# Sliding-window attention and a two-layer block on one core: the fourth tile of keys and queries transposed by DMA, and the loads of tiles 4 and 5 issued after two GpSimd copies

## The chip, the core and the metric

The kernel runs on one core of a Trainium2 chip. The metric is the device time of one execution in microseconds; the kernel before has been run eight times, and the median of those runs is what a change is compared with. One further view, the profile, is taken of one of these executions.

## The reference, cut to what matters

```
q, k, v: (8, 8, 576, 64) float32           # batch, heads, sequence, head dimension
scores = q @ k^T / 8, only where |i - j| <= 32, then softmax, then @ v
x = attention output as 4608 tokens x 512
h = x @ w_in                                # 512 -> 2048
g = h * sigmoid(1.702 h)
out = g @ w_out                             # 2048 -> 512
```

## The kernel before, in words

**Units and windows.** The 4608 tokens are one long row, cut into 36 units of 128 tokens. A window w handles two units of attention (2w and 2w+1), the first layer for the units of the window before it (`layer1(w-1, ...)`), and the second layer for the units of two windows before. The order of instructions on every engine is the order in which the program writes them[...]. `head()` is a hand-written start for units 0 to 6, `window(4)` is a written-out transition, and from window 5 on `window(w)` repeats, one window after the other, until `close`. In the steady part the second layer is a Strassen-like set of seven products (`product`, line 394) whose sums are made by VectorE (`g_sums`).

**Keys and queries.** Attention needs keys and queries transposed, head dimension on the partitions: `kT` (a ring of 1536 keys, with 64 wrapped columns behind it, from `RING` on) and `qT` (the same for queries, 384 columns for each of four interleaved positions, with wrapped columns from `RP` on). They come in tiles of 512 tokens: tile 3 is tokens 1536 to 2047, and it lands at the start of the ring again. Its first 64 keys are the last ones that unit 11 needs, and unit 11 reads them from the wrapped columns. There are two ways from DRAM to `kT`:

- By TensorE: `load_heads` (line 138) brings rows of 256 values, `pair_heads` (a `cast`, line 106) puts two heads side by side, `heads_T` (line 176) transposes on TensorE into PSUM, and `keys_T` and `queries_T` copy out of PSUM (line 106 again). Tiles A, B, 1, 2 and 3 go this way.
- By DMA: `load_keys` (line 146) brings rows of 64 values, and `keys_X` (line 151) is a DMA transpose of 128 tokens at a time, from the SyncE queue. For queries `load_heads` and `pair_heads` stay, and `queries_X` (line 221) is one DMA transpose of the whole tile. Tiles 4 to 8 go this way.

**Queues.** All loads with a cast from float32 are issued by GpSimd, in program order: `load_v` (line 157), `load_keys`, `load_heads`. SyncE issues all DMA transposes, the stores of the output (lines 349 and 423), and `x_T` (line 315), the transpose of the attention output that layer 1 multiplies. An instruction that waits on either of these two engines holds all that stand behind it. Staging tiles `ks` and `qs` have three buffers each, `p` five, `xT` four.

**Order around the change.** At the end of `head`, GpSimd copies tile 2 side by side, then loads values 8 to 10, tile 3, values 11 to 13, and tile 4. In window 4 TensorE computes scores 7, 8 and 9, the second layer of units 4 and 5, values 7 to 9, and layer 1 of window 3 (eight pieces), between which stand the transposes of tile 3. `loads()` near the middle brings values 14 and 15 and tile 5. At the end of window 4 and 5 `feed` issues `keys_X(4, ...)`, makes the shifted copies of values (`odd_v`) and, in window 5, the side-by-side queries of tile 4 and `queries_X(4)`. Window 6 starts with `loads()` for tile 6.

Of the kernel before, what the change touches and what calls it, by code (L numbers as in the profile page):

```python
# [22 lines left out]
JT = 4  # L23
NV = 8
RING = 1536
RP = RING // JT


class _Kernel:
# [410 lines left out]
    def head(self):  # L440

        nc, dve, act, pool = self.nc, self.nc.vector, self.nc.scalar, self.nc.gpsimd
# [125 lines left out]
        self.load_v(8)  # L568
        self.load_v(9)
        self.load_v(10)  # L570
        for c in "kq":
            self.load_heads(3, c)
        self.layer1(2, 0)
        self.values(6)
        self.norm(6)
# [13 lines left out]
            self.odd_v(m, dve)  # L589
        for m in (11, 12, 13):  # L590
            self.load_v(m)
        self.load_keys(4)
        self.load_heads(4, "q")

    def window(self, w):
        nc, dve, sp = self.nc, self.nc.vector, self.nc.sync
        a, b = 2 * w, 2 * w + 1
        att = w < self.NW
        t, act = w - 2, nc.scalar
        l1 = [(lambda d=d: self.layer1(w - 1, d)) for d in range(8)] if w <= self.NW else []  # L600

        def run(lst, n=1):
            for _ in range(min(n, len(lst))):
                lst.pop(0)()

        def loads():
            for m in (2 * w + 6, 2 * w + 7):
                if m < self.NU:
                    self.load_v(m)
            if w % 2 == 0 and 512 * (w // 2 + 3) < self.N:  # L610
                self.load_keys(w // 2 + 3)
                self.load_heads(w // 2 + 3, "q")

        if w == 4:
            l2 = [(lambda u=u, i=i: self.layer2(u, i, "oh"[u % 2], (dve, act)[u % 2])) for u in (4, 5) for i in range(4)]
            self.scores(7)
            self.scores(a)
            run(l2, 3)
            self.band(7)
            self.scores(b)  # L620
            run(l2)
            self.band(a)
            self.values(7, "th")
            self.gelu_table()
            for m in (10, 11):
                self.odd_v(m, act)
            self.band(b)
            self.norm(7)
            run(l2, 2)
            self.values(a)  # L630
            self.values(b)
            run(l2)
            self.x_T(7, "t", nc.scalar)
            self.norm(a)
            self.x_T(a)
            self.norm(b)
            self.x_T(b)
            run(l2)
            loads()
            run(l1, 2)  # L640
            for c in "qk":
                for hp in range(4):
                    self.pair_heads(c, 3, hp, dve)
            run(l1, 2)
            for hp in range(4):
                self.keys_T(3, hp)
                self.queries_T(3, hp, "a", nc.scalar)
                run(l1)
            self.g_sums(w - 1, 0)
            self.feed(w)  # L650
            return
        loads()
        if not att:
            self.close(w, l1)
            return
        self.scores(a)
        if w > 5:
            self.scores(b)
        self.g_sums(t, 1, (0, 1))
        self.product(t, 1, "o")  # L660
        self.keep(t, 1, dve)
        self.product(t, 2, "h")
        if w == 5:
            self.scores(b)
        self.g_sums(t, 1, (2, 3))
        self.result(t, 11)
        self.gelu_table()
        self.product(t, 5, "t")
        self.band(a)
        self.product(t, 6)  # L670
        self.band(b, 0)
        self.keep(t, 6, dve)
        self.band(b, 1)
        run(l1)
        self.values(a)
        self.values(b)
        self.norm(a)
        self.x_T(a)
        self.product(t, 7)
        self.keep(t, 7, dve)  # L680
        self.result(t, 22)
        run(l1, 1)
        self.product(t, 4)
        self.result(t, 21, act)
        self.norm(b)
        self.x_T(b)
        self.product(t, 3)
        self.result(t, 12)
        run(l1, len(l1) - 4)
        self.g_sums(w - 1, 0)  # L690
        self.feed(w)
        run(l1, 4)
# [36 lines left out]
    def feed(self, w):  # L729

        dve = self.nc.vector
        if w % 2 == 0:
            self.queries_wrap((w + 2) // 2)
        for m in (2 * w + 2, 2 * w + 3):
            if 11 < m < self.NU:
                self.odd_v(m, dve)
        i = (w + 4) // 2
        if 512 * i < self.N:
            if w % 2:
                if 512 * i % RING == 0:  # L740
                    dve.tensor_copy(self.kT[:, :, RING:], self.kT[:, :, 0:64])
                for hp in range(4):
                    self.pair_heads("q", i, hp, dve)
                self.queries_X(i)
            for c in ((2, 3) if w % 2 else (0, 1)):
                self.keys_X(i, c)
        if w == 16:
            dve.tensor_copy(self.kT[:, :, RING:], self.k_first)
            dve.tensor_copy(self.qT[:, :, RP:RP + 8], self.q_first)

    def run(self):
        self.head()
        for w in range(4, self.NW + 2):
            self.window(w)
# [47 lines left out]
```

## Time and profile before

| | |
|---|---|
| median of 8 runs | 297.7 us (295.8 to 300.29) |
| the execution that was profiled | 300.29 us, span 298.4 us |
| TensorE matmul busy | 288.4 us, 97% of the span |
| VectorE, ScalarE, GpSimd busy | 195.3, 189.6 and 86.8 us |
| DMA, all queues | 37.78 MB, 118,650 packets |
| time of one steady window | 14.61 us (from the scores at 129.08 to those at 143.69) |

The profiled execution is the slowest of the eight, so what it shows of stalls need not be in every run. Busy time of an engine is the time in which an instruction of it ran; a transfer's landing time is counted from its issue to the last byte's arrival. "SPq" is SyncE as the issuer of transfers, and a line such as `L106` is shared by every copy of the kernel, so it is told apart by the tiles that it writes and reads.

### The profile page before, as it was taken

The numbers are of one execution on the slowest core, as the hardware profiler recorded it, in microseconds if no ns is written. First come the engines' busy times: TensorE is split into PE (matmuls) and PEld (weight loads), VectorE is DVE, ScalarE is ACT, GpSimd is POOL, SyncE is SP. The second block draws the span as 40 slices with busy tenths as digits, with TensorE's granted clock in tenths as the row PEclk, the third lists the DMA queues.
The fourth block names the chain that finished last, engine by engine and source line by source line (L and its number), as shares of the span: only waits on it lengthen the run. The fifth ranks groups of instructions, "written<-read, shape, count | busy, mean of one in ns | idle before, by whom it ended". The sixth has DMA issues, their size and how long they took to land.

```text
span 298.4 us, 9587 instructions
## 1 busy us (share of the span) xinstructions
PE 288.4 (97%) x4050; PEld 236.9 (79%) x4052; DVE 195.3 (65%) x584; ACT 189.6 (64%) x314; POOL 86.8 (29%) x127
## 2 busy tenths in 40 slices
PE   7999999999999987999999999999999999999995
PEld 2578665866888875888888888888888888888884
DVE  3662468678786754595759686867686758683352
ACT  4676467698866665384849494848585757575330
POOL 8884525967365200902080202011100000000000
PEclk9999999999999998999999999999999999999999
DMA  9999999999999999999499959691953030303012
GB/s 145 156 207 205 200 184 167 159 165 191 124 166 142 166 121 162 119 182 147 124 114 189 161 107 143 90 164 34 141 110 105 2 109 3 108 2 105 2 70 73
DMA packets 118650, 37.78 MB, mean 127 GB/s; under 512 B 96080, under 2 KB 114256, under 8 KB 118608
## 3 DMA queue, kind: packets, MB, share of 16 engines
q0 software_dynamic: 75888, 18.16, 74.5%
q1 hardware_dynamic: 42272, 18.62, 32.8%
q8 instruction: 32, 0.52, 0.8%
q10 hardware_dynamic: 448, 0.39, 0.5%
q14 instruction: 10, 0.08, 0.1%
HBM read 36.96 MB, written 9.44 MB: 155 GB/s over the span
## 4 chain that ended last, share of the span: by engine, by line
PE 90%; DMA 5%; POOL 2%; DVE 1%; issue 1%; ACT 0%; POOLq 0%; DVEq 0%
PE h_ps L332 43%; PE o_ps L394 30%; PE o_ps L344 7%; PE pv L292 4%; PE sc L263 4%; DMA xT<-x 2%; DMA qs<-in_q_dram 2%; PE tp L176 2%; POOL ve L157 1%; PE tp L319 0%; POOL ks L138 0%; DVE o_sb L412 0%; POOL neg L237 0%; DVE kT L106 0%; ACT qT L106 0%
## 5 line engine op out<-in xcount | busy, mean ns | idle before, releaser
L332 PE MATMUL h_ps<-xT,w_in_sb 128*128 128x256 bf16 x1152 | 136.4, 273 | 2.1 <-DMA xT<-x 2.0
L334 ACT ACTIVATE g<-h_ps 128x512 f16<-128x512 f32 x144 | 85.5, 596 | 78.1 <-PE h_ps L332 76.8
L332 PEld LDWEIGHTS <-w_in_sb 128*128 128x128 bf16 x1152 | 112.2, 98 | 16.0 <-issue 2.6
L157 POOL DMA_DIRECT2D ve<-in_v_dram x40 | 33.9, 859 | 100.0 <-PE pv L292 83.9
L394 PEld LDWEIGHTS <-gs 128*128 128x128 f16 x480 | 46.1, 98 | 6.0
L394 PE MATMUL o_ps<-w_sum,gs 128*128 128x256 f16 x360 | 44.8, 275 | 0.0
L269 ACT ACTIVATE p<-sc 128x512 bf16<-128x512 f32 x72 | 37.2, 604 | 2.7 <-PE sc L263 2.5
L394 PEld LDWEIGHTS <-g 128*128 128x128 f16 x360 | 34.2, 98 | 4.5 <-ACT g L334 0.2
L371 DVE TENSOR_TENSOR gs<-g 128x512 f16<-128x512 f16 x30 | 12.7, 422 | 31.6 <-ACT g L334 30.9
L304 DVE TENSOR_TENSOR x<-pv,rec 128x256 bf16<-128x256 f32 x72 | 30.6, 424 | 2.7 <-DVE rec L303 0.2
L394 PE MATMUL o_ps<-w_out_sb,g 128*128 128x256 f16 x240 | 29.1, 273 | 0.0
L106 DVE COPY part<-o_ps 128x256 f32<-128x256 f32 x45 | 19.1, 424 | 13.5 <-PE o_ps L394 12.3
L412 DVE TENSOR_TENSOR o_sb<-o_ps,part 128x256 f32<-128x256 f32 x45 | 19.0, 422 | 12.1 <-PE o_ps L394 11.4
L281 DVE TENSOR_TENSOR p<-p,mask 128x512 bf16<-128x512 bf16 x64 | 24.3, 422 | 0.6 <-ACT p L269 0.6
L344 PE MATMUL o_ps<-w_out_sb,g 128*128 128x512 f16 x96 | 23.2, 380 | 0.0
L106 DVE COPY vo<-ve 64x528 bf16<-64x528 bf16 x61 | 19.0, 312 | 3.1 <-DMA ve<-in_v_dram 1.7
L303 DVE RECIPROCAL rec<-pv 128x4 f32<-128x4 f32 x72 | 12.6, 175 | 12.7 <-PE pv L292 12.5
L146 POOL DMA_DIRECT2D ks<-in_k_dram x22 | 18.8, 874 | 2.4 <-DMA qs<-in_q_dram 1.0
L431 ACT ACT_TABLE_LOAD x15 | 19.2, 1283 | 0.3
L269 ACT ACT_TABLE_LOAD x15 | 19.2, 1283 | 0.3
L292 PEld LDWEIGHTS <-p 128*64 128x64 bf16 x576 | 11.5, 113 | 6.2 <-DVE p L281 3.4
L263 PEld LDWEIGHTS <-kT 64*64 64x64 bf16 x1152 | 11.8, 107 | 5.7 <-issue 5.3
(69 smaller groups left out, 263.6 us busy)
## 6 DMA issues: line engine op xcount, KB each, us to landing
out_dram<-o_sb SPq DMA_DIRECT2D x34, 256.0 KB, 2.8
ve<-in_v_dram POOLq DMA_DIRECT2D x32, 128.0 KB, 6.2
ks<-in_k_dram POOLq DMA_DIRECT2D x19, 128.0 KB, 8.4
w_in_sb<-in_moe_w_in_dram POOLq DMA_DIRECT2D x4, 512.0 KB, 11.1
w_out_sb<-in_moe_w_out_dram POOLq DMA_DIRECT2D x4, 512.0 KB, 12.6
qs<-in_q_dram POOLq DMA_DIRECT2D x2, 448.0 KB, 11.8
qs<-in_q_dram POOLq DMA_DIRECT2D x3, 256.0 KB, 7.3
qs<-in_q_dram POOLq DMA_DIRECT2D x2, 384.0 KB, 13.0
```

The source lines that it names most:

```text
L106: (eng.copy if eng is self.nc.scalar else eng.tensor_copy)(out, in_)
L157: self.nc.gpsimd.dma_start(self.ve[m % NV][off:off + n, :, :self.D], self.v[b, :, s:s + n, :].rearrange("h s d -> s h d"))
L263: nc.tensor.matmul(sc[eo][lo:lo + 64, 2 * hp + blk, :], self.kT[r, hp, at:at + 64], self.qT[r, JT * hp:JT * hp + JT, q0:q0 + 16], start=(s ...
L269: nc.scalar.activation(p[:, eo].rearrange("k h (s j) -> k h s j", j=JT), sc[eo].rearrange("k h (j s) -> k h s j", j=JT), AF.Exp, scale=sel ...
L281: self.nc.vector.tensor_mul(pv, pv, msk.to_broadcast([128, 4, 2, SQ]))
L292: nc.tensor.matmul(acc[half][blk * 64:blk * 64 + 64, hh, :], p[:, h % 2, h // 2 * 2 + blk, :], vt[:, h, :D + 1], start=(hh == 0), stop=(hh ...
L304: nc.vector.tensor_mul(x[:, hs, :], acc[half][:, :, :D], rec[:, hs, :].to_broadcast([128, 4, D]))
L332: nc.tensor.matmul(hps[:, i, :], self.w_in_sb[:, kr, ff * 128:(ff + 1) * 128], self.xT[t][:, kr, :], start=(i == 0 and kr == 0), stop=(i = ...
L334: nc.scalar.activation(self.g[t][:, ffs[0]:ffs[1] + 1:ffs[1] - ffs[0], :], hps, AF.Gelu_apprx_sigmoid)
L344: nc.tensor.matmul(o_ps, self.g[t][:, ff, s * 128:(s + 1) * 128], self.w_out_sb[:, ff, :], start=(ff == 0), stop=(ff == self.NFF - 1))
L394: nc.tensor.matmul(self.part[t, key], x, y, start=(first and k == 0), stop=(k == 7), skip_group_check=True)
L431: self.nc.scalar.activation(self.spark, self.spark, AF.Gelu_apprx_sigmoid)
```

## The change

Tile 3 goes the second way. In `head`, `load_keys(3)` takes the place of `load_heads(3, "k")`, and the four `keys_X(3, c)` stand at the end. The loads of tile 4 leave `head`. In window 4, ScalarE makes the side-by-side queries of tile 3 where it made the shifted values 10 and 11 (VectorE makes those later, where it made the side-by-side keys and queries). SyncE then issues `queries_X(3)`. GpSimd makes the two wrapped copies, of 64 columns of `kT` and 8 of each row of `qT`, and only after them come the loads: values 14 and 15, tile 4, tile 5. The transposes on TensorE of tile 3 and the copies out of PSUM are gone, and `feed(4)` no longer makes the wrapped copy of queries on VectorE.

```diff
@@ head
-        for c in "kq":
-            self.load_heads(3, c)
+        self.load_keys(3)
+        self.load_heads(3, "q")
...
         for m in (11, 12, 13):
             self.load_v(m)
-        self.load_keys(4)
-        self.load_heads(4, "q")
+        for c in range(JT):
+            self.keys_X(3, c)
@@ window: loads()
-            if w % 2 == 0 and 512 * (w // 2 + 3) < self.N:
-                self.load_keys(w // 2 + 3)
-                self.load_heads(w // 2 + 3, "q")
+            for i in ((4, 5) if w == 4 else (w // 2 + 3,) if w % 2 == 0 else ()):
+                if 512 * i < self.N:
+                    self.load_keys(i)
+                    self.load_heads(i, "q")
@@ window 4
             self.gelu_table()
-            for m in (10, 11):
-                self.odd_v(m, act)
+            for hp in range(4):
+                self.pair_heads("q", 3, hp, act)
+            self.queries_X(3)
+            self.nc.gpsimd.tensor_copy(self.kT[:, :, RING:], self.kT[:, :, 0:64])
+            self.nc.gpsimd.tensor_copy(self.qT[:, :, RP:RP + 8], self.qT[:, :, 0:8])
+            loads()
             self.band(b)
...
             run(l2)
-            loads()
-            run(l1, 2)
-            for c in "qk":
-                for hp in range(4):
-                    self.pair_heads(c, 3, hp, dve)
-            run(l1, 2)
-            for hp in range(4):
-                self.keys_T(3, hp)
-                self.queries_T(3, hp, "a", nc.scalar)
-                run(l1)
+            for m in (10, 11):
+                self.odd_v(m, dve)
+            run(l1, 8)
             self.g_sums(w - 1, 0)
             self.feed(w)
@@ feed
-        if w % 2 == 0:
+        if w % 2 == 0 and w > 4:
             self.queries_wrap((w + 2) // 2)
```

## The prediction

> **What bounds the kernel now.** I read the page first, then the chain of waits around the one place where TensorE stops, then the SyncE queue and the DMA shares there.
>
> ```profile
> span 298.4 us, 9587 instructions
> PE 288.4 (97%) x4050; PEld 236.9 (79%) x4052; DVE 195.3 (65%) x584; ACT 189.6 (64%) x314; POOL 86.8 (29%) x127
> ...
> PE   7999999999999987999999999999999999999995
> ...
> PEclk9999999999999998999999999999999999999999
> DMA  9999999999999999999499959691953030303012
> ```
>
> TensorE is full in all slices but the first, the last and two at 112 to 127 us, where its clock dips too. DMA is full until about 149 us. So the kernel is bound by TensorE, and the DMA engines are the threat in the first half. The critical chain from 105 us shows the dip:
>
> ```profile
> 104.92 4.58 PE h_ps L332 x42
> 109.51 7.43 DMA xT<-x
> 116.93 0.14 issue
> 117.07 1.71 PE h_ps L332 x8
> ```
>
> The busy times by stretch, there (TensorE's matmuls, weight loads, VectorE, ScalarE, GpSimd, then granted clock, DMA share, GB/s):
>
> ```profile
> 115.00:117.00 2.00, 0.04 (x1) 0.00 (x0) 0.76 (x2) 0.14 (x1) 0.00 (x0) 1.00 0.93 163
> 117.00:119.00 2.00, 1.93 (x20) 1.26 (x22) 0.00 (x0) 0.19 (x1) 0.00 (x0) 0.57 0.55 122
> 119.00:121.00 2.00, 2.00 (x38) 1.64 (x33) 1.12 (x4) 0.41 (x1) 1.35 (x2) 0.58 0.03 8
> ```
>
> TensorE waits from 115.04 to 117.07 for the transposed x of unit 13, issued at 109.51, and then runs at 0.57 of its clock for some 3.4 us. Window 7 takes 129.08 - 109.55 = 19.53 us instead of 14.61: 4.9 us lost, which includes 1.0 us of waiting for `qT` at 110 us. Why is that transpose late? The SyncE queue:
>
> ```profile
> 70.65 2.70 SPq L315 DMA_TRANSPOSE xT<-x  x2
> ...
> 74.08 5.59 SPq L151 DMA_TRANSPOSE kT<-ks  x2
> 87.04 1.19 SPq L315 DMA_TRANSPOSE xT<-x  x1
> ...
> 89.75 1.28 SPq L315 DMA_TRANSPOSE xT<-x  x1
> ...
> 95.90 6.41 SPq L221 DMA_TRANSPOSE qT<-qc  x1
> 102.40 4.55 SPq L151 DMA_TRANSPOSE kT<-ks  x2
> 107.04 1.74 SPq L315 DMA_TRANSPOSE xT<-x  x1
> ...
> 109.51 1.87 SPq L315 DMA_TRANSPOSE xT<-x  x1
> ```
>
> The queries of tile 4 landed 15.1 us after their issue, and everything behind them slid: the whole string from 95.90 to the last landing took 21.0 us. The DMA counts say what it shared with: from 101 to 112 us GpSimd's queue moved 3024 packets and SyncE's 2762; from 112 to 118 GpSimd's moved 206 and SyncE's 2868. The string caught up only when the loads ran dry.
>
> **What the Trainium skill says.** "DMA: Bandwidth & Descriptors", section "Queues, rings and completion order", says that each DMA engine takes turns between the queues that have work, packet by packet. The trace agrees that the two share: two key transposes beside a full load queue landed after 10.7 us, against 2.5 us for the quickest. The same page, "Anatomy of one DMA", says that a transfer's semaphore wait is held by the issuing sequencer; so a wait of GpSimd or SyncE holds all behind it, as the in-order rows above show. "TensorE: Matmul & The Clock Gate", part 1, gives an idle window of about 3.4 us as what halves the clock; here 2.03 us of idling sufficed and 1.0 us (at 110 us) did not, so the measurement decides, and I price a second long stop at 1.7 us (half of 3.4).
>
> **The change part by part.**
>
> *Removed from TensorE:* the 32 transposes of tile 3, in the chain four pieces "0.45 PE tp L176 x8" between layer-1 pieces: 4 x 0.45 = 1.8 us, all on the path, since TensorE is full there. Certain gain: 1.8 us. Off the path: on VectorE eight side-by-side copies (2.5 us) and eight copies of keys out of PSUM (3.3 us); on ScalarE four of queries (2.3 us). In their place VectorE gets four shifted copies of values (1.3 us) and ScalarE four side-by-side copies for 2.59 us of value copies, nearly equal. VectorE and ScalarE have room in window 4; nothing.
>
> *Added load:* `load_keys(3)` has 512 x 8 = 4096 pieces of 128 bytes where `load_heads` had 1024. Loads of such pieces ran at 2677 packets in 3 us (55 to 58), so 4.6 us against about 3.0 (0.52 MB at the 175 GB/s of 85 to 90 us). GpSimd issues five transfers of 0.88 for two of 0.69 us: 3.0 us more ahead of queries 3 and values 11 to 13. Tile 4's load no longer follows, so these still land by about 68 us, when ScalarE wants the queries (its value copies started at 68.14). Nothing; up to 1 us if they slip.
>
> *Added transposes:* four `keys_X(3)` and `queries_X(3)`, together 4096 packets of 256 bytes. At 2868 packets in 6 us, alone on the engines, 8.6 us of transfer. The keys fall at 60 to 70 us; queries are issued when ScalarE is done, 68.14 + 2.4 = 70.5, with GpSimd's queue dry, and land after 4.3 (best) to 7.3 us (median of `qT`): I take 5, 75.6 us. The x transposes of units 8 and 9 slide from 70.65 to about 73 and are wanted at 84.49 - 1.8. Nothing.
>
> *The new wait:* GpSimd's two copies stand behind these. GpSimd's 128x512 copies took 0.6 us; these have 256 and 128 elements, so an estimated 0.8 for both: done at about 76.5. Scores 11 want them at 82.36 - 1.8 = 80.6: 4 us to spare. Nothing on the path, but queued behind the copies are all loads from value 14 on. At 76.75 GpSimd before had issued everything through keys 5 (72.55 + 4.20). After, it begins there: values 14 and 15 (2.3 us at the 892 per us above), keys 4 (4.6), queries 4 (3.0), keys 5 (4.6), 14.5 us of transfer, of which before still had some 5 to move. So the load queue lags by 9 us from there. The engines idled little before 118 us, so the lag isn't made up by then.
>
> *Where it is paid, first:* `keys_X(4, 0)` and `(4, 1)` wait for keys 4, issued at 78.3 to 80 us and landing near 82 to 84 (2.6 to 5 us for small loads on a fresh queue); before they had been issued at 74.08. Their 1024 packets now stand right ahead of the x of units 10 and 11. From 77 to 85 us SyncE's queue got 1765 packets in 8 us, 221 per us: 4.6 us, until about 87, with x of unit 10 due out at 85.2. So that string is 1.9 us later. Unit 11's x landed at 89.75 + 8.8 = 98.55 against 99.11 when layer 1 wanted it: 0.6 to spare, so 1.3 us of stop. Bounds: 0 (no delay) and 4.0.
>
> *Second:* the string from `queries_X(4)` to unit 13's x. It starts 1.8 earlier with TensorE and 1.9 later by the above. In its last 5 us (112 to 117) it no longer drains alone: some 1850 packets that are left (2868 without the 1024 of the next keys) go at 2762/11 = 251 per us, 7.4 us instead of 5: +2.4. Bounds: 0 and the whole lag, 9. So TensorE resumes at 117.07 - 1.8 + 1.9 + 2.4 = 119.6, 2.5 us later than before, with the first stop contained in that. A second halving of the clock after the first stop, 1.3 us being between the 1.0 that did not and the 2.0 that did: half of 1.7, 0.9. Window 8 has 5 us to spare for its x (issued 123.83, landing 4.2 later, wanted at 133.34): nothing, up to 2.
>
> *Sum:* +2.5 + 0.9 = +3.4 us; 300.29 + 3.4 = 303.7 for the profiled execution. That one lies 2.6 above the median and has the whole 4.9 of window 7, about the width of all eight runs, so other runs lose less there. I carry the difference over: 297.7 + 3.4 = 301.1, say 301.0. A measurement of this kernel can tell about 1% from no change, 294.7 to 300.7.
>
> **The rivals.**
>
> *First, not slower: the transposes keep their turn.* If SyncE's queue gets its share whatever waits in the other, the lag of the loads costs nothing, since they are prefetches, and both stops stay as they were: 297.7 - 1.8 = 295.9. If the gap in the loads at 67 to 76 us lets the strings run freely and window 7's stop goes too, 300.29 - 1.8 - 4.9 = 293.6. For it: x of units 10 and 11 landed in time beside full loads. Against it: queries 4 took 15.1 us, and from 98 to 101 us SyncE's queue got 100 packets of 2975. It decides from the point where unit 13's x lands less than 2 us after TensorE's new want, 113.2.
>
> *Second, slower still: scores 11 wait for the wrapped copies.* If queries 3 land as late as queries 4 did, 70.5 + 15.1 + 0.8 = 86.4 against 80.6: 5.8 us stop, the loads slipping with it, 301.1 + 5.8 = 306.9. For it: a full chain of load, ScalarE, transpose, GpSimd. Against: GpSimd's queue is dry just then.
>
> **How the numbers follow.** Main case 0.50 (of which 0.08 end within 1%), first rival 0.40 (0.13 of it faster by over 1%, 0.27 within), second 0.10. So faster 0.13, same 0.35, slower 0.52. Range: down to 294.0 (the stop gone), up to 306.0 (first stop at its bound, 2.7 more, and 2 of window 8). The main case alone spans 299 to 305.
>
> **What would show it.** Right: no `tp<-ident,kc` after 71 us; window 5's scores begin near 78.4; loads silent between about 67 and 76 us; a wait for xT near 97 us and a longer one near 114. Wrong: unit 13's x landing by 115 with full loads beside it (the share argument fails), a wait of `sc` at 80 us (second rival), or stops in window 4.

## The result, and the profile after

The changed kernel has a median of 306.78 us over 11 runs (301.24 to 310.25), the kernel before 297.4 us over 32. The ratio is 1.0215, with a 95% interval of 1.0154 to 1.0276. It leaves out each kernel's runs that lie more than 1.5% above its fastest, eight of the changed kernel's and the profiled execution of each kernel among them; the two medians take in all runs and lie further apart (1.032). The forecast was 301.0 us, in a range of 294.0 to 306.0. The ratio alone would put the changed kernel at 304.1 us (1.0215 times 297.7), inside the range; the median of all its runs lies above it. The profiled execution took 308.21 us; its page and slices:

```profile
span 306.5 us, 9523 instructions
PE 290.4 (95%) x4018; PEld 237.2 (77%) x4020; DVE 190.5 (62%) x571; ACT 187.6 (61%) x310; POOL 89.6 (29%) x132
...
PE   7989999999999399999599999999999999999995
...
PEclk9979999999999799999969999999999999999999
DMA  9999996999999999999999996793845030303012
```

Where one dip stood in the slices of 104 to 119 us (the prediction read them as 112 to 127), there are now two, near 100 and near 150 us, each with a dip of the clock at it. A third dip of the clock, at 15 to 23 us, is new too. TensorE's rows at the ends of the two, with the idle time before them and its releaser in brackets:

```profile
104.49 1.87 PE L332 MATMUL h_ps<-xT,w_in_sb 128*128 128x256 bf16 x8 [5.54 <-DMA xT<-x]
...
153.49 1.89 PE L332 MATMUL h_ps<-xT,w_in_sb 128*128 128x256 bf16 x8 [3.70 <-DMA xT<-x]
```

Both wait for an x transpose. The first is that of unit 11, which layer 1 wants in window 6, the second that of unit 17, wanted in window 9. Eight matmuls took 1.87 us where such a row takes 1.04 (before, at 75.20): the granted clock is 0.50 from 104.40 to 106.40 us, and again from 153.40 to 155.40.

A table of windows, each from the start of its first scores on TensorE's timeline to that of the next, says where the 8.1 us between the two spans lie:

| | before | after | difference |
|---|---|---|---|
| start to scores 7 | 61.55 | 63.22 | +1.67 |
| window 4 | 18.58 | 16.60 | -1.98 |
| window 5 | 14.80 | 14.80 | 0 |
| window 6 | 14.62 | 21.61 | +6.99 |
| window 7 | 19.46 | 14.62 | -4.84 |
| window 8 | 14.61 | 14.61 | 0 |
| window 9 | 14.61 | 20.86 | +6.25 |

They sum to 8.09 us. (The prediction's 19.53 for window 7 took its end from another view.) Windows 6 and 9 lost more than their stops of 5.54 and 3.70 us, and the clock is the rest: behind the two stops it stayed at half until 107.5 and 158.7 us, 3.0 and 5.2 us of TensorE's work, of which half, 1.5 and 2.6 us, is lost.

The start isn't the change's. The clock was at half there from 18.8 to 22.2 us, and 3.4 us at half the clock are 1.7 us. In the fourteen traces of this case, the seven with such a halving near 20 us reach scores 7 at 63.22 to 64.35 us, and the seven without it at 61.55 to 62.38. Three of those without it carry the change (61.69, 61.91 and 62.38), and one of those with it is a kernel whose start and window 4 are those of the kernel before (63.34, the run with the key transposes of every tile later). Its slices of the clock show the dip:

```profile
PEclk9979999999999999999999999999999999999998
```

Why the clock halves there in some executions was not looked into.

The chain in GpSimd's and SyncE's timelines shows how window 6 comes to stop. First GpSimd, with its two copies at lines 629 and 630:

```profile
71.54 0.40 POOL L629 COPY kT<-kT 128x256 bf16<-128x256 bf16 x1 [6.60 <-DMA kT<-ks]
79.93 0.29 POOL L630 COPY qT<-qT 128x128 bf16<-128x128 bf16 x1 [7.98 <-DMA qT<-qc]
80.44 1.76 POOL L157 DMA_DIRECT2D ve<-in_v_dram  x2 [0.22 <-issue]
82.19 3.53 POOL L146 DMA_DIRECT2D ks<-in_k_dram  x4
```

and SyncE:

```profile
71.89 4.52 SPq L221 DMA_TRANSPOSE qT<-qc  x1
76.50 3.56 SPq L315 DMA_TRANSPOSE xT<-x  x2
...
87.48 3.36 SPq L151 DMA_TRANSPOSE kT<-ks  x2
90.94 1.35 SPq L315 DMA_TRANSPOSE xT<-x  x1
...
93.05 1.28 SPq L315 DMA_TRANSPOSE xT<-x  x1
...
95.81 9.27 SPq L221 DMA_TRANSPOSE qT<-qc  x1
```

The queries of tile 3 land 8.0 us after their issue; the engines are not free for them, since values 11 to 13 land from 73.1 to 75.8 us and tile 3's own key transposes from 71.5 to 75.1. The copies end at 80.2, the keys of tile 4 are issued at 82.19 and land 5.2 us later, and so SyncE can't go past `keys_X(4, 0)` before 87.48. The x of units 10 and 11 stand behind it, 3.9 and 3.3 us later than before (87.04 and 89.75), although TensorE was 0.3 us ahead of before there (scores 12 at 94.62 against 94.93). And the x of unit 11 then takes 11.3 us to land instead of 8.8.

### The profile page after: what moved, and what is told of

The parts are those of the page before. It is cut to its first block, busy times and chain, and to the rows that moved or that the text cites. A ratio compares the mean times of both kernels' runs of the same rounds, so it can differ in the third digit from the quotient of the medians.

```text
span 306.5 us, 9523 instructions
## 1 busy us (share of the span) xinstructions
PE 290.4 (95%) x4018; PEld 237.2 (77%) x4020; DVE 190.5 (62%) x571; ACT 187.6 (61%) x310; POOL 89.6 (29%) x132
## 4 chain that ended last, share of the span: by engine, by line
PE 86%; DMA 9%; DVE 2%; ACT 1%; issue 0%; SPq 0%; DVEq 0%
PE h_ps L332 40%; PE o_ps L394 28%; DMA xT<-x 7%; PE o_ps L344 7%; PE pv L292 4%; PE sc L263 4%; PE tp L176 2%; DMA k_raw<-in_k_dram 1%; PE tp L319 1%; DVE x L304 1%; ACT qT L106 0%; PE sc L245 0%; ACT g L334 0%; PE junk L437 0%; DVE kc L106 0%
## 5 line engine op out<-in xcount | busy, mean ns | idle before, releaser
L332 PE MATMUL h_ps<-xT,w_in_sb 128*128 128x256 bf16 x1152 | 138.5, 277 | 9.3 <-DMA xT<-x 9.2
L332 PEld LDWEIGHTS <-w_in_sb 128*128 128x128 bf16 x1152 | 113.5, 99 | 24.6 <-issue 5.8
L371 DVE TENSOR_TENSOR gs<-g 128x512 f16<-128x512 f16 x30 | 12.7, 422 | 35.4 <-ACT g L334 35.4
L146 POOL DMA_DIRECT2D ks<-in_k_dram x27 | 22.8, 874 | 9.2 <-DMA qs<-in_q_dram 4.3
L394 PE MATMUL o_ps<-w_sum,g 128*128 128x256 f16 x120 | 15.6, 272 | 0.0
```

The costliest lines, as they stand in the source:

```text
L146: self.nc.gpsimd.dma_start(kn[off:off + n, c], self.k[b, :, s:s + n, :].rearrange("h s d -> s h d"))
L332: nc.tensor.matmul(hps[:, i, :], self.w_in_sb[:, kr, ff * 128:(ff + 1) * 128], self.xT[t][:, kr, :], start=(i == 0 and kr == 0), stop=(i = ...
L394: nc.tensor.matmul(self.part[t, key], x, y, start=(first and k == 0), stop=(k == 7), skip_group_check=True)
```

## The experiments

Each ran beside the kernel before on the same chip. Ratios have their 95% intervals beside them; "loses" is a window's length less 14.61 us.

### Tile 4 ahead of the copies

```diff
+            for m in (14, 15):
+                self.load_v(m)
+            self.load_keys(4)
+            self.load_heads(4, "q")
             self.nc.gpsimd.tensor_copy(self.kT[:, :, RING:], self.kT[:, :, 0:64])
             self.nc.gpsimd.tensor_copy(self.qT[:, :, RP:RP + 8], self.qT[:, :, 0:8])
-            loads()
+            self.load_keys(5)
+            self.load_heads(5, "q")
```

> The changed kernel, with the loads of values 14 and 15 and of tile 4 ahead of GpSimd's two copies; only tile 5 stays behind them. Theory A (tile 4 comes late, its key transposes hold SyncE's queue, and the x of units 10 and 11 stand behind them): keys 4 land before 80 us, SyncE issues the x of unit 10 near 87 again, and the 5.5 us stop of window 6 falls under 1.5 us; time about 1.00 to 1.01 of before. Theory B (the added transposes and their traffic slow every x transpose, whenever tile 4 is loaded): the stop of window 6 stays at 4 us or more and the time at about 1.02. A price either way: the queries of tile 3 are transposed beside loads and land later than the 8.0 us of the changed kernel, so scores 11 may wait up to 4 us.

Measured: 307.14 us, 1.0369 (1.0296 to 1.0443). SyncE had finished with the keys of tile 4 before it came to the x of unit 10, and window 6 lost 0.35 us: that part of theory A holds. Its time was wrong all the same. The queries of tile 3 landed after 13.6 us, and scores 11 waited for GpSimd's copy:

```profile
86.13 0.41 PE L263 MATMUL sc<-qT,kT 64*64 64x64 bf16 x28 [3.60 <-POOL qT L634]
```

Window 5 lost 5.9 and window 7 8.8 us. With tile 4's loads not held, the loss moves to other windows; it doesn't go.

### Holding alone

```diff
         for m in (11, 12, 13):
             self.load_v(m)
-        self.load_keys(4)
-        self.load_heads(4, "q")
...
                 self.queries_T(3, hp, "a", nc.scalar)
                 run(l1)
+            self.nc.gpsimd.tensor_copy(self.qT[:, :, RP:RP + 8], self.qT[:, :, 0:8])
+            loads()          # tiles 4 and 5, as in the changed kernel
```

The `loads()` further up in window 4 and the wrapped copy on VectorE go.

> The kernel before, tile 3 transposed on TensorE as it was, but tiles 4 and 5 are loaded in window 4 behind one GpSimd copy (the wrapped queries) that waits for ScalarE's last queries of tile 3, near 80 us. Theory A (holding the loads is the cost): windows 6 and 9 stop as in the changed kernel, 5 to 6 us each, and the time is that of the changed kernel plus the 1.8 us of transposes that TensorE keeps: 1.02 to 1.035 of before. Theory B (the added transposes are the cost): no such stop, 0.99 to 1.01.

Measured: 311.41 us, 1.0479 (1.0409 to 1.0549), the slowest of all and above what was expected. The GpSimd copy ran at 82.55, SyncE came to the keys of tile 4 at 90.05, and TensorE stopped in the same two windows:

```profile
106.78 1.89 PE L332 MATMUL h_ps<-xT,w_in_sb 128*128 128x256 bf16 x8 [5.01 <-DMA xT<-x]
...
157.07 1.86 PE L332 MATMUL h_ps<-xT,w_in_sb 128*128 128x256 bf16 x8 [3.94 <-DMA xT<-x]
```

Window 6 lost 7.2 and window 9 6.5 us, against 7.0 and 6.25 in the changed kernel, with no added transpose anywhere. Held loads suffice for both stops. The spans of the two traces are 3.6 us apart (310.1 and 306.5 us), 2.0 of it in window 4, where the transposes stay on TensorE.

### Keys of tile 4 behind the x

```diff
         self.x_T(b)
+        if w == 5:
+            for c in (0, 1):
+                self.keys_X(4, c)
...
-            for c in ((2, 3) if w % 2 else (0, 1)):
+            for c in ((2, 3) if w % 2 else (0, 1) if w > 4 else ()):
```

> The changed kernel, with the first two key transposes of tile 4 issued behind the x of unit 11 instead of ahead of the x of unit 10. Theory A: SyncE issues the x of unit 10 near 87 and of unit 11 near 89.5 instead of 90.94 and 93.05; the stop of window 6 falls from 5.5 to 2 us or less, the stop of window 9 stays; time 1.00 to 1.015 of before. Theory B (shared engines, not the order): x of unit 11 still lands after 102 us, and the time stays at 1.02.

Measured: 303.08 us, 1.0209 (1.0131 to 1.0288). SyncE's timeline has the x at 87.12 and 89.80, as theory A said, and window 6 lost 0.05 us. But window 7 now lost 8.5 us:

```profile
112.03 0.41 PE L263 MATMUL sc<-qT,kT 64*64 64x64 bf16 x28 [1.91 <-DMA qT<-qc]
...
120.09 1.86 PE L332 MATMUL h_ps<-xT,w_in_sb 128*128 128x256 bf16 x8 [4.05 <-DMA xT<-x]
```

and the stop of window 9, which I had expected to stay, was gone. SyncE's order says which window pays. That an amount of transfer is late as a whole behind it is a reading, which this run alone doesn't show. The ratio is that of the changed kernel (1.0215): nothing was gained that the runs can tell.

### Tile 5 at the start of window 5

The loads of tile 5 move from behind tile 4 to the start of window 5.

> The changed kernel, with tile 5 loaded at the start of window 5, behind values 16 and 17, instead of right behind tile 4. Theory A (SyncE's wait for keys 4): x of unit 10 is still issued near 91, and the stop of window 6 shrinks by less than 1.5 us. Theory C (the x of unit 11 lands in 11.3 us because tile 5's keys run beside it): values 16 and 17 are in place of them, nearly the same traffic at that time; if it shrinks by more than 2.5 us, the amount loaded back to back is what counts. Time 1.01 to 1.025.

Measured: 307.62 us, 1.0358 (1.0296 to 1.0421). The x of unit 10 was issued at 91.32, the stop of window 6 was 3.46 us instead of 5.54, between what the two theories said, and window 9 lost 6.8 us. The time is above the expected range: moving tile 5 alone by so little gains nothing.

### The added transposes alone

```diff
             self.scores(7)
+            for c in range(JT):
+                nc.sync.dma_start_transpose(self.kT[:, :, 512 + 128 * c:640 + 128 * c], ...)   # from tile 3's staged keys
...
+            nc.sync.dma_start_transpose(self.qT[:, :, 128:256], ...)                            # from tile 3's staged queries
```

> The kernel before with its tile 3 on TensorE and its loads where they were, plus the five transposes that the change adds (four of 128 tokens, one of a whole tile), issued by SyncE at the same places but into the ring's place of tile 4, where nothing reads them before tile 4 overwrites it. Theory B (traffic and queue time of the added transposes cost by themselves, some 4 us in window 4 to 7): stops of together 5 us more than before, time 1.015 to 1.03. Theory A (only the held loads cost): no more than 1 us more than before, 1.00 to 1.005.

Measured: 303.63 us, 1.0228 (1.0182 to 1.0273): theory B's figure. The whole-tile transpose held SyncE for 8.64 us beside the loads of tile 4 and landed after 14.9; the x of units 8 and 9 stood behind it:

```profile
70.47 8.64 SPq L630 DMA_TRANSPOSE qT<-qs  x1
79.21 2.88 SPq L315 DMA_TRANSPOSE xT<-x  x2
```

Layer 1 of window 5 waited 4.66 us for the x of unit 9, and the window lost 6.2 us. So both parts of the change cost when done alone, each more than the 1.8 us that TensorE saves. They do not add: in the changed kernel tile 4's loads do not run beside the queries of tile 3, which land after 8.0 us, and window 5 loses only the 0.2 us that it lost before.

### The key transposes of every tile later, in the kernel before

```diff
         self.x_T(b)
+        i = (w + 3) // 2
+        if w % 2 == 0 and 512 * i < self.N:
+            for c in (2, 3):
+                self.keys_X(i, c)
...
-            for c in ((2, 3) if w % 2 else (0, 1)):
+            for c in (() if w % 2 else (0, 1)):
```

> The kernel before with the third and fourth key transposes of each tile issued one window later, behind the x of the next odd unit, instead of between the queries and the x of the next even unit. If SyncE's order is what makes the x of unit 13 late (the string of 21.0 us from the queries of tile 4), it lands some 4.5 us earlier, the 2.0 us stop of window 7 goes and the time is 0.985 to 0.995 of before. If the shared DMA engines alone set it, 0.998 to 1.002.

Measured: 296.56 us, 1.0012 (0.9986 to 1.0038). No stop was left in window 7 (it lost 0.15 us), so the order does make the x of unit 13 late. The time did not follow. The second look below says why in part: there the stop is shorter. But it still cost 1.7 us in that execution, and this run's median shows none of it; the lowest times with and without the move are level (295.52 and 295.53 us). In the trace itself the gain went at the two ends, which the move doesn't touch: scores 7 began 1.8 us later than in the first trace of before, and from the last matmul to the end of the kernel it was 5.4 us instead of 3.7.

> The kernel before, unchanged, for a second trace. If the start (scores 7 at 61.55 us before, 63.22 after) differs for the change's sake, scores 7 start near 61.5 again; if it is an execution's own state, anywhere from 61.5 to 64.5. The stop of window 7 is expected in this one too if the execution is near 300 us, and not if it is near 296.

A second execution of the kernel before, at 297.52 us, stopped for 1.21 us and lost 1.7 us in window 7, not 4.9; scores 7 began at 61.73. My profile of before had been an extreme one, and the stop on which I built cost about a third as much in this one.

### Both moves in the changed kernel

Keys 0 and 1 of tile 4 behind the x of unit 11, keys 2 and 3 of each tile behind the x of the next odd unit.

> The changed kernel with both moves: the first two key transposes of tile 4 behind the x of unit 11, and the third and fourth of each tile behind the x of the next odd unit. By the order theory the 8.5 us that window 7 lost in the run with the first move alone shrink to some 4 us, of which the wait for the queries of tile 4 (1.9 us) stays; time 0.99 to 1.01 of before. If the engines' traffic alone decides, it stays at 1.02.

Measured: 301.46 us, 1.0143 (1.0091 to 1.0196), a little above what the order theory gave. In the trace, of an execution of 303.49 us, window 7 lost 3.3 us and window 6 1.5; stops appeared as late as windows 10 and 11 (1.1 and 3.9 us lost). TensorE pays in many places for transfers that are late.

### The keys alone

Tile 3's keys by DMA, its queries on TensorE, no load held.

> Half of the change: the keys of tile 3 by the second way (loaded by load_keys, four DMA transposes at the end of head, wrapped copy on VectorE), its queries on TensorE as before, and no load held back: tile 4 is loaded at the end of head as before. TensorE saves half of 1.8 us, 0.9. If the price of the change is mainly the whole-tile transpose of the queries (8.6 us in SyncE's queue in the run with the added traffic alone) and the held loads, this one is at 0.995 to 1.003 of before. If any added transpose beside the loads costs, there are stops for the x of units 8 to 13 of 2 us or more and the time is 1.005 to 1.015.

Measured: 307.55 us, 1.0349 (1.031 to 1.0387), far outside both. The larger part that can be told from before is a third cause, in window 4. ScalarE makes the shifted values 10 and 11 here, as before, and the values that they need were issued at 61.31, behind the keys' smaller pieces, and landed 12.7 us later; ScalarE's copy of the x of unit 7 stood behind them. The waits of 62 to 88 us:

```profile
PE h_ps L332 <- ACT xT L106: 3.3, 1, 3.3
ACT vo L106 <- DMA ve<-in_v_dram: 3.3, 1, 3.3
```

Window 4 took 22.61 us instead of 18.58. The changed kernel avoids this by giving those copies to VectorE later: its values land as late (73.1 us against 74.0), without tile 4's loads, and its ScalarE goes on. Window 7 lost 5.4 us as well, with a stop of 2.73 us for the x of unit 13, where the two traces of the kernel before lost 4.9 and 1.7; how much of that is due to the added key transposes is open.

> As the run with the keys of tile 3 alone, and the third and fourth key transposes of each tile one window later, behind the x of the next odd unit. By itself that move was worth nothing measurable (1.001). If the two meet (the added transposes push the string of tile 4), it takes back what the keys alone cost: 0.993 to 1.0; if not, the same as the keys alone.

With the later keys as well: 302.05 us, 1.0162 (1.0117 to 1.0207), between the two expectations: the stop in window 4 is still there (window 4 took 21.82 us), and window 7 lost 1.3 us instead of 5.4.

### Tiles loaded one window later

The kernel with both moves, and

```diff
-            for i in ((4, 5) if w == 4 else (w // 2 + 3,) if w % 2 == 0 else ()):
+            for i in ((4,) if w == 4 else (w // 2 + 3,) if w % 2 else ()):
```

> The changed kernel with the key transposes behind the x (as in the run that had both moves, 1.014 of before), and tile 5 loaded at the start of window 5, tile 6 at 7, tile 7 at 9, tile 8 at 11, one window later than before. If the prefetches of tiles 5 and 6 right behind tile 4 are what slows the queries of tile 4 and the x of unit 13, the stop of window 7 goes below 1 us and the time is 0.99 to 1.005. If not, 1.01 to 1.02, with stops elsewhere.

Measured: 297.93 us, 1.0016 (0.999 to 1.0041). Window 7 still lost 3.1 us, which was not foreseen, but the later windows were free of stops but for 0.2 us. The time of the kernel before is reached.

### No loads beside the transposed queries

```diff
-            for i in ((4, 5) if w == 4 else (w // 2 + 3,) if w % 2 == 0 else ()):
+            for i in ((4,) if w == 4 else ((w + 3) // 2,) if w % 2 and w > 5 else ()):
...
         self.x_T(b)
+        i = (w + 3) // 2
+        if 512 * i < self.N:
+            for c in ((0, 1) if w % 2 else (2, 3)):
+                self.keys_X(i, c)
...
-            for c in ((2, 3) if w % 2 else (0, 1)):
-                self.keys_X(i, c)
```

The wrapped copy of the keys moves into the even windows with them.

> The changed kernel, with tile 4 behind the copies as it is, but tiles 5 to 8 loaded at the start of windows 7, 9, 11 and 13, behind values that wait for TensorE, and all key transposes behind the x of the odd unit of the window after. So no load of keys or queries runs while the queries of a tile are transposed at the end of an odd window. If the order of the two queues' traffic is the whole cost of the change, the queries of tile 4 land within 8 us of their issue, window 7 loses under 1 us, and the 1.8 us saved on TensorE are left: 0.988 to 0.996 of before. If the added transposes cost by themselves, 1.0 to 1.01.

Measured: 295.93 us against 297.17, 0.9955 (0.9926 to 0.9984): clearly faster than the changed kernel, and a little faster than the kernel before, by less than the 1% that the prediction thought could be told. Behind the start its slices have one faint dip, and the clock none:

```profile
PE   8889999999999799999999999999999999999994
PEclk9999999999999999999999999999999999999999
```

and its longest stop, on TensorE's timeline:

```profile
100.05 1.03 PE L332 MATMUL h_ps<-xT,w_in_sb 128*128 128x256 bf16 x8 [1.78 <-DMA xT<-x]
```

Window 7 lost nothing. The queries of tile 4 landed after 11.2 us, more than the 8 that I had allowed, without harm; what is left of a stop is the x of unit 11 in window 6 (2.1 us lost), beside the loads of tile 4 and of the values behind them. The added transposes and the change's saving on TensorE are all in this kernel, so the transposes as such need not cost time: when the loads run and where the key transposes stand decides. The key transposes behind the x alone gave 1.0143, with the loads one window later 1.0016; what this run's two further moves do singly was not separated. How the kernel before would do with its loads moved in the same way was not run, so the 0.45% can't be divided between the saving and the moved loads.

## Why the prediction was right or wrong

**Right: the direction, the saving, and the first half of the path.** Window 4 is 1.98 us shorter; I had 1.8. The loads lag, SyncE comes late to the x behind the keys of tile 4, unit 11 stops TensorE, and the removed work on VectorE and ScalarE brought nothing. Run alone, the hold makes the stops. The second string slipped as I had priced it, too: the x of unit 13 landed at 119.84 us, 2.9 us later than before (116.93), and I had TensorE resume on it at 119.6. But TensorE didn't want it yet.

**Wrong: the size, and the places.** I had +3.4 us on the profiled execution; its windows say +6.4 without the start (8.1 - 1.67), the ratio of 1.0215 is 6.4 us too, and the medians are 9.4 apart. Three terms:

*The first stop, "1.3 us", was 5.54.* The estimate that the queries of tile 3 land in 5 us was wrong: 8.0. I had GpSimd's queue dry just then, with values 11 to 13 landed by about 68 us; they landed from 73.1 to 75.8. The copies ended at 80.2, not at 76.5 (1.7 us of that is the later start). I had put `keys_X(4, 0)` near 82 to 84 and only counted its packets as an obstacle to the x of unit 10. It was issued at 87.48, so the wait itself held SyncE, 3.9 us for unit 10. That stands nowhere in the sum, though the prediction itself says that a wait of SyncE holds all behind it. And the x of unit 11 took 2.5 us longer to land than before, where I had carried its 8.8 us over. My upper bound of 4.0 us missed the stop.

*The second stop, "+2.4", was not in window 7.* Window 7 lost nothing, since window 6 had held TensorE back by 7.0 us while the string from the queries of tile 4 went on (95.81, as before at 95.90). I had said that the later stop contains the earlier; it was the other way round. By the end of window 8 the change had cost 0.2 us (-1.98 + 6.99 - 4.84) against the first trace of before, and 3.3 against the second, in which window 7 lost less. That 3.3 is near the sum's 3.4 is chance, since other terms make it up. For the clock I had 0.9 us more than before; it was 1.5 in window 6 and 2.6 in window 9, less some 1.7 in window 7.

*Window 9 has no term in the sum, and lost 6.25 us.* I stopped at window 8 ("nothing, up to 2"; it lost nothing), and priced its x against its slack as before, with the load queue as it was before; but the loads were still late. GpSimd came to the keys of tile 7 at 128.22 us, before at 121.88. The DMA counts of 126 to 150 us, before and after (packets, MB, and the time that the packets took as a share of the 16 engines' span):

```profile
q0 software_dynamic: 5867, 1.13, 72.1%
q1 hardware_dynamic: 6422, 2.41, 57.2%
```

```profile
q0 software_dynamic: 10715, 1.94, 111.1%
q1 hardware_dynamic: 5113, 1.77, 61.6%
```

GpSimd's queue moved 10,715 packets where it had moved 5,867, beside the transposed queries of tile 5 (11.6 us to land) and the x of unit 17 (10.7 us). In the kernel before, the queries of tile 5 had taken 7.3 us. As I read it, a stop of TensorE gives the DMA engines time, but also delays the waits on TensorE that release the loads (the values ahead of tile 7 waited for TensorE until 127.07), so the lag was carried further and met the next string. No run tested that by itself.

**The rivals.** The first, that the transposes keep their turn whatever waits in the other queue, is refuted for this kernel: the x of units 10 and 11 landed after 9.5 and 11.3 us, before after 7.9 and 8.8, and the stops did not stay as they were. As a statement of what is possible it was near: with the traffic reordered, a kernel with the added transposes stands at 0.9955. The second, scores 11 waiting for the wrapped copies, did not happen in the changed kernel (80.2 against 82.05) and did, for 3.60 us, where tile 4 was not held; holding the loads is what prevents it. Its sum, 306.9 us, lies by the median of 306.78, which is chance: that wait isn't in the changed kernel.

**Left open.** How the DMA engines divide their time between the two queues was not measured by itself; the runs show landing times under mixed traffic, no rule. Why the spread of times of one kernel is so wide (301.24 to 310.25) is not settled either; the mean granted clock goes with it (0.992 at 301.24 us, 0.976 at 310.25), and by an estimate from these two figures the clock makes up some 5 of the 9 us.

## What to carry to other kernels

When transfers share engines with other transfers, holding a prefetch back is not free of charge: count what stands behind the held loads, which in-order queue waits for them next, and at which later point the lag meets the next dense stretch. A stop moved by reordering one queue came back in the next window until the other queue's loads were moved too. And price a stall from more than one execution: the one that I started from lost 4.9 us in a window where another lost 1.7.

## What the runs showed of the hardware that was not expected

In the fourteen traces, from 25 us on, all fifteen stops of TensorE's matmuls of 2.03 us or more had the granted clock at half behind them, and none of the nine of 0.93 to 1.91 us had. The halving doesn't begin with the stop's end: it began from 2.4 us before to 1.3 us after TensorE resumed, so the first eight matmuls can still run at full clock. The six shortest that had it:

| stop | run | clock at half, after TensorE resumed | for |
|---|---|---|---|
| 2.03 us | before | 0.2 us | 3.4 us |
| 2.06 us | both moves in the changed kernel | 1.2 us | 3.4 us |
| 2.51 us | the keys alone, and key transposes later | 1.1 us | 3.4 us |
| 2.73 us | the keys alone, window 7 | 1.1 us | 3.4 us |
| 3.29 us | the keys alone, window 4 | 0.3 us | 3.4 us |
| 3.46 us | tile 5 at the start of window 5 | 0.7 us | 3.4 us |

After the nine longer ones (3.60 to 5.88 us) it lasted 3.4 us three times and 6.8 us six times. Half of the time that TensorE then works at half the clock is lost on top of the stop. The issue of one whole-tile transpose occupied SyncE for anything from 1.3 us (where it landed after 6.7) to 9.3 us (where it landed after 16.1), and everything behind it on SyncE waited for that.
